# Weight rounding shared out by step, attention products moved and loads reordered in the first part of an attention and mixer kernel, and two products and some sums moved in the second

## The chip, the cores and the metric

One core of one Trainium2 chip. The metric is the device time of one execution in microseconds (us), lower is better. A kernel is executed several times and the median is quoted. Each comparison is made with executions of the kernel before on the same chip in the same rounds.

Ratios are computed as the mean time of one kernel's fast runs over the mean time of the other's fast runs of the same rounds, so they are not quite the ratio of the medians that are quoted. The brackets behind a ratio are its 95% interval.

## The reference, cut to what matters

```python
# 8 batches, 8 heads, 576 positions, head dimension 64; all in float32
kv  = einsum('bhsd,bhse->bhde', k, v)
out = einsum('bhsd,bhde->bhse', q, kv)
x   = out / sqrt(mean(out*out, -1) + 1e-6) * g_norm      # then heads side by side: (8, 576, 512)
# token mixing, w_tok1 (576, 256), w_tok2 (256, 576)
h = maximum(x.transpose(0, 2, 1) @ w_tok1, 0) @ w_tok2
u = x + h.transpose(0, 2, 1)
# channel mixing, w_ch1 (512, 1536), w_ch2 (1536, 512)
result = u + maximum(u @ w_ch1, 0) @ w_ch2
```

The four weight matrices arrive as float64, two 32-bit words for each value. The kernel has to turn them into float32 itself.

## The kernel before

The kernel has two parts. The first does attention and token mixing and stores `u`. It works on pairs of batches: after the attention of the first pair, a loop of three passes puts the attention of the next pair beside the token mixing of the last, and one more token mixing ends it. The second part does the channel mixing of nine groups, with two levels of fast matrix products (seven products instead of eight).

The steps of the first part have short names: `kv00` to `kv11` (k^T v of one batch, half of the heads), `a0` to `a3` (q times kv, with the norm), `r` (the 64 positions left over), `h00` to `h11` and `hr` (first token layer), `u0` to `u8` (second). The program issues them in a fixed order, and every engine works through its own instructions in that order.

A `kv` step ends with two short copies that pack the block for the next products, one on VectorE and one on ScalarE:

```python
def kv(side, half):
    acc = ps["kv"].tile([P, 2, P], F32, name="ps_kv")          # one such buffer
    ...                                                        # 20 matmuls
    keep(nc.vector.tensor_copy(dst[:HF, :, :D], acc[:HF, :, :D]))
    copy(dst[HF:, :, D:], acc[HF:, :, D:])                     # ScalarE
    load(n + 4)
```

An `a` step squares its product on ScalarE at once and leaves the rest for later (`due`): `mean` (VectorE's reduction, then the root on ScalarE) in the first half of the filling of its own step, `divide` in the second half, the gain on GpSimd after the next step:

```python
def mean():
    keep(nc.vector.tensor_reduce(ms, x3, axis=AX.X, op=ALU.add))
    ...
    keep(nc.scalar.activation(root, ms, AF.Sqrt))
def divide():
    ...
    keep(nc.vector.tensor_mul(x3, o, inv.to_broadcast([P, n * H, D])))   # frees ps_o, the one buffer
def gain(t):
    keep(nc.gpsimd.tensor_mul(xt, xt, g_sb.to_broadcast([P, H, D])))
```

The rounding of one block of weights is three fill steps. The first costs VectorE nothing; each of the others has one VectorE instruction with one input from SBUF and one with two:

```python
def scale():    # ScalarE L162, GpSimd L163
    keep(nc.scalar.activation(dst, hi.bitcast(F32), AF.Copy, scale=2.0 ** -112))
    keep(nc.gpsimd.tensor_scalar(out=dst, in0=dst, scalar1=TOP, scalar2=-TOP, op0=ALU.min, op1=ALU.max))
def upper():    # VectorE L168, L170
    keep(nc.vector.tensor_scalar(out=bits, in0=bits, scalar1=3, ..., op0=ALU.logical_shift_left))
    keep(nc.vector.scalar_tensor_tensor(out=bits, in0=hi, scalar=0x80000000, in1=bits, ...))
def lower():    # VectorE L176, L178, GpSimd L118
    keep(nc.vector.tensor_scalar(out=part.bitcast(U32), in0=bits, scalar1=0xFF800000, ...))
    keep(nc.vector.scalar_tensor_tensor(out=part, in0=lo, scalar=2.0 ** -52, in1=part, ...))
    tensor_add(dst, dst, part, engine=nc.gpsimd)
```

These fill steps are laid behind the steps of the loop, evenly:

```python
def run(body, fill):
    for n, step in enumerate(body):
        step()
        upto = len(fill) * (n + 1) // len(body)
        ...          # the fill steps up to `upto`, in two halves, each followed by what is due
```

In the profile, L127 is the helper through which every matmul goes, L118 that of the additions, L121 that of the relus, L124 that of ScalarE's copies, L283 VectorE's copy of kv, L298 the mean, L310 the multiplication that ends a norm. PSUM is the memory of this kernel's `ps_` tiles, SBUF that of its other tiles. A group of matmuls is called cold when it ran at a lower granted clock and so took longer than the same group elsewhere (4.64 us against 2.50 for the 20 matmuls of a `kv`), and warm otherwise.

## Time and profile before

| Stage of the profiled run | us |
|---|---|
| start: attention of the first pair | 0 to 53 |
| three passes of the loop | 53.6, 61.8, 60.6 |
| last token mixing | 40.6 |
| channel mixing, nine groups | 659.7 |
| whole (median of 3 runs 928.79, 928.31 to 930.03) | 929.3 |

The views behind this table are shown in the prediction. They are to be read by stage: in the channel mixing TensorE is busy nearly all the time, so only the few waits in it can be won. In the first part TensorE is busy 50 to 54 us of passes that take up to 61.8. What stands between is time in which it waits for a buffer or a packed block, plus the slow matmuls that follow some of the waits.

### The profile page before, as it was taken

What the parts mean: (1) busy time and instruction counts of PE and PEld (TensorE: products, weight loads), DVE (VectorE), ACT (ScalarE), POOL (GpSimd) and SP (SyncE); (2) the same over time, 40 slices, a digit from 0 to 9 for tenths busy, and PEclk for the clock granted to TensorE, in tenths of its full rate; (3) what the DMA queues carried; (4) which work ended last, traced back from release to release, by engine and by line L of the source; (5) the groups of instructions that cost most, each with busy time, mean ns of one, the idle gap of its engine ahead of it and who ended that gap; (6) DMA issues with size and microseconds to landing.
All of it is one profiled execution on the core that took longest, in us unless ns stands there. A gap on an engine that the chain in (4) does not pass through costs nothing.

```text
span 929.3 us, 12432 instructions
## 1 busy us (share of the span) xinstructions
PE 864.5 (93%) x5136; PEld 735.6 (79%) x5136; DVE 566.6 (61%) x862; ACT 175.8 (19%) x300; POOL 279.9 (30%) x164
## 2 busy tenths in 40 slices
PE   4589798898979998999999999999999999999997
PEld 4566365564458888889989989989989989989986
DVE  2747948769886577636726736636646646546652
ACT  2212122131201101301301311211310310220210
POOL 1534434444430003502502601700700800800710
PEclk9689989899989999999999999999999999999999
DMA  9976657715330011002002002002002002001001
GB/s 295 342 237 192 225 159 227 236 52 180 104 125 1 1 39 53 1 1 91 1 1 91 1 1 92 1 1 91 1 1 91 1 1 89 3 1 46 1 1 45
DMA packets 43576, 72.53 MB, mean 78 GB/s; under 512 B 2688, under 2 KB 21120, under 8 KB 43520
## 3 DMA queue, kind: packets, MB, share of 16 engines
q1 hardware_dynamic: 42160, 70.53, 23.0%
q10 hardware_dynamic: 1360, 1.21, 0.4%
q8 instruction: 40, 0.66, 0.3%
q14 instruction: 16, 0.13, 0.0%
HBM read 52.85 MB, written 18.87 MB: 77 GB/s over the span
## 4 chain that ended last, share of the span: by engine, by line
PE 78%; DVE 13%; issue 3%; ACT 2%; DMA 2%; SPq 0%; ACTq 0%; DVEq 0%
PE ps_w L127 34%; PE ps_v L127 31%; PE ps_h L127 6%; PE ps_kv L127 3%; DVE w_ch L170 2%; PE ps_o L127 2%; DMA v_in<-in_v_dram 2%; DVE x L118 2%; DVE ms L298 2%; PE ps_ut L404 2%; ACT v L121 1%; DVE w_ch L168 1%; DVE part L176 1%; DVE uT L118 1%; DVE x L310 1%
## 5 line engine op out<-in xcount | busy, mean ns | idle before, releaser
L127 PE MATMUL ps_v<-uT,w 128*128 128x128 f32 (+1 forms) x1656 | 213.2, 282 | 5.2 <-DVE uT L118 5.2
L127 PEld LDWEIGHTS ps_v<-uT,w 128*128 128x128 f32 x1656 | 200.9, 194 | 8.0 <-issue 5.6
L118 POOL TENSOR_TENSOR vs<-vs,v 128x1536 f32<-128x1536 f32 x8 | 27.7, 3467 | 422.9 <-DVE vs L118 422.9
L127 PE MATMUL ps_v<-uT,w_ch 128*128 128x128 f32 (+1 forms) x864 | 124.6, 287 | 4.0 <-DVE u L118 4.0
L127 PEld LDWEIGHTS ps_v<-uT,w_ch 128*128 128x128 f32 x864 | 112.7, 192 | 8.2 <-DVE u L118 4.4
L127 PE MATMUL ps_w<-w_ch,v 128*128 128x256 f32 x432 | 97.0, 381 | 5.6 <-ACT v L121 5.6
L127 PE MATMUL ps_w<-d,vs 128*128 128x256 f32 x432 | 96.2, 379 | 0.0
L127 PE MATMUL ps_w<-w_ch,vs 128*128 128x256 f32 x432 | 96.2, 379 | 0.0
L127 PEld LDWEIGHTS ps_w<-w_ch,v 128*128 128x128 f32 x432 | 80.8, 190 | 17.5 <-ACT v L121 7.1
L118 DVE TENSOR_TENSOR vs<-ps_v,u 128x384 f32<-128x384 f32 (+1 forms) x123 | 69.0, 561 | 39.3 <-PE ps_v L127 30.4
L127 PEld LDWEIGHTS ps_w<-w_ch,vs 128*128 128x128 f32 x432 | 81.5, 190 | 10.7
L127 PEld LDWEIGHTS ps_w<-d,vs 128*128 128x128 f32 x432 | 80.8, 190 | 10.3
L124 ACT COPY t<-ps_v 128x384 f32<-128x384 f32 (+1 forms) x59 | 28.6, 485 | 208.8 <-PE ps_v L127 196.6
L127 PEld LDWEIGHTS ps_kv<-v_in,k_in 128*128 128x128 f32 x320 | 44.7, 224 | 28.3 <-ACT kvp L124 11.4
L127 PE MATMUL ps_kv<-v_in,k_in 128*128 128x128 f32 x320 | 47.2, 312 | 21.4 <-DMA v_in<-in_v_dram 11.9
L127 PE MATMUL ps_u<-h,w_tok 128*128 128x512 f32 (+1 forms) x160 | 66.4, 602 | 0.0
L127 PE MATMUL ps_h<-x,w_tok 128*128 128x512 f32 (+1 forms) x160 | 66.2, 610 | 0.0
L118 DVE TENSOR_TENSOR u<-ps_v,t 128x384 f32<-128x384 f32 (+1 forms) x59 | 33.3, 565 | 46.1 <-PE ps_v L127 45.9
L118 POOL TENSOR_TENSOR w_ch<-w_ch,part 128x384 f32<-128x384 f32 (+1 forms) x28 | 35.1, 1254 | 84.3 <-DVE part L178 84.3
L118 POOL TENSOR_TENSOR v<-v,vs 128x1536 f32<-128x1536 f32 x16 | 55.3, 3454 | 12.9 <-DVE v L118 8.9
L118 DVE TENSOR_TENSOR u<-ps_w,u 128x512 f32<-128x512 f32 x18 | 12.5, 692 | 73.6 <-PE ps_w L127 73.6
L118 DVE TENSOR_TENSOR uT<-uT 128x512 f32<-128x512 f32 (+1 forms) x68 | 56.6, 874 | 0.6
(74 smaller groups left out, 995.1 us busy)
## 6 DMA issues: line engine op xcount, KB each, us to landing
qT<-in_q_dram SPq DMA_DIRECT2D x8, 1152.0 KB, 7.4
xg<-u_dram SPq DMA_DIRECT2D x9, 1024.0 KB, 5.7
k_in<-in_k_dram SPq DMA_DIRECT2D x16, 512.0 KB, 5.6
u_dram<-x SPq DMA_DIRECT2D x16, 512.0 KB, 3.1
out_dram<-xg SPq DMA_DIRECT2D x16, 512.0 KB, 2.8
v_in<-in_v_dram SPq DMA_DIRECT2D x14, 512.0 KB, 6.7
raw<-in_moe_w_ch_dram SPq DMA_DIRECT2D x16, 384.0 KB, 6.6
raw<-in_moe_w_ch_dram SPq DMA_DIRECT2D x12, 512.0 KB, 4.3
```

The source lines that it names most:

```text
L118: keep(engine.tensor_tensor(out=o, in0=a, in1=b, op=op))
L121: keep(nc.scalar.activation(o, a, AF.Relu))
L124: keep(nc.scalar.copy(o, a))
L127: keep(nc.tensor.matmul(*a, **kw))
L168: keep(nc.vector.tensor_scalar(out=bits, in0=bits, scalar1=3, scalar2=None, op0=ALU.logical_shift_left))
L170: keep(nc.vector.scalar_tensor_tensor(out=bits, in0=hi, scalar=0x80000000, in1=bits, op0=ALU.bitwise_and, op1=ALU.bitwise_or))
L176: keep(nc.vector.tensor_scalar(out=part.bitcast(U32), in0=bits, scalar1=0xFF800000, scalar2=None, op0=ALU.bitwise_and))
L298: keep(nc.vector.tensor_reduce(ms, x3, axis=AX.X, op=ALU.add))
L310: keep(nc.vector.tensor_mul(x3, o, inv.to_broadcast([P, n * H, D])))
L404: keep(nc.tensor.transpose(pt[:, c], xg[g][:, i, ts(c, P)], ident))
```

## The change

Its intent is to let VectorE do as much rounding in the loop as there is room for, in the steps where there is room, and to take away waits of TensorE. It has five parts:

1. The loads of k, v and q of the second pair go ahead of those of the token weights.
2. Rounding is shared out by step instead of evenly: six shares to an `h` step, four to a `kv`, one to a `u`, none to `a` and `r`. The loop rounds 27 blocks instead of 24, so three are left for the last token mixing instead of six. The three blocks rounded before the loop stand behind `r` and `a2` now, and no longer behind the steps from `a0` to `kv11`.
3. The attention products stand further apart among the other steps, and `a3` of the first pair moves behind the first `h00`.
4. In the channel mixing the order of two of the seven outer products, 5 and 2, is exchanged, with their relus.
5. The last eight sums of channel weights are done in the first group instead of the second.

Cut to its core:

```diff
-    ORDER = (1, 6, 7, 5, 2, 3, 4)
+    ORDER = (1, 6, 7, 2, 5, 3, 4)
 ...
-    def run(body, fill):
+    def run(body, fill, shares=None):
+        shares = shares or [1] * len(body)
 ...
-            upto = len(fill) * (n + 1) // len(body)
+            upto = len(fill) * sum(shares[:n + 1]) // sum(shares)
 ...
-    second = "h00 kv00 h01 kv01 a0 h10 h11 hr kv10 a1 kv11 u0 u1 r u2 a2 u3 u4 u5 u6 a3 u7 u8"
+    middle = ("h10 h11 a1 hr kv10 u0 kv11 u1 a2 u2 r u3 u4 u5 a3 u6 u7 u8").split()
+    second = "h00 kv00 h01 kv01 a0".split() + middle
 ...
+    share = {"h": 6, "k": 4, "u": 1, "a": 0, "r": 0}
 ...
-    for n in (0, 1, 2):
-        blocks[n][0]()            # loads of token weights
-    load(2)
-    load(3)
-    load_q(1)
-    for n in (3, 4):
-        blocks[n][0]()
+    for n in range(2, 4):
+        load(n)
+    load_q(1)
+    for n in range(5):
+        blocks[n][0]()
 ...
-    run(steps[2:6], [blocks[0][1], blocks[1][1]] + weights[:9])
+    run(steps[:6], [])
+    run(steps[6:], [b[1] for b in tok1] + [f for b in tok1 for f in b[2:]])
 ...
-    cut = 3 * 27
-    run(steps, weights[9:cut])
+    cut = 3 * 27 + 2
+    names = ["h00", "a3"] + second[1:] + 2 * both
+    run([...], weights[:cut], [share[name[0]] for name in names])
 ...                                # channel mixing, first group
-            weave([...], sums[:-8])
+            weave(body[:11], sums)
```

More of the change, by code (lines that the diff above doesn't have):

```diff
@@ L526, in after5 @@
             padd(s3, s3, s1)
-            relus.append((3, do(relu, a22, a22)))
+            relus.append((4, do(relu, a22, a22)))
         def after2():
             padd(a11, a11, s4)
-            relus.append((4, do(relu, a11, a11)))
+            relus.append((3, do(relu, a11, a11)))
         def after4():
@@ L665, in staggered @@
     def staggered(blocks, ahead=5):
-        steps = []
+        steps = [blocks[0][1], blocks[1][1]]
         for n, (_, _, upper, lower) in enumerate(blocks):
@@ L702 @@
                       ap=[[0, P], [0, 1], list(g_norm.ap[0])]), nc.scalar)
-    first = "kv00 kv01 a0 kv10 a1 kv11 r a2 a3"
-    second = "h00 kv00 h01 kv01 a0 h10 h11 hr kv10 a1 kv11 u0 u1 r u2 a2 u3 u4 u5 u6 a3 u7 u8"
-    both = "kv00 h00 kv01 h01 a0 h10 h11 hr kv10 a1 kv11 u0 u1 r u2 a2 u3 u4 u5 u6 a3 u7 u8"
+    first = "kv00 kv01 a0 kv10 a1 kv11 r a2"
+    middle = ("h10 h11 a1 hr kv10 u0 kv11 u1 a2 u2 r u3 u4 u5 a3 u6 u7 u8").split()
+    second = "h00 kv00 h01 kv01 a0".split() + middle
+    both = "kv00 h00 kv01 h01 a0".split() + middle
     last = "h00 h01 h10 h11 hr u0 u1 u2 u3 u4 u5 u6 u7 u8"
+    share = {"h": 6, "k": 4, "u": 1, "a": 0, "r": 0}
     blocks = ([get_tok1(0, 2), get_tok1(2, 2), get_tok1(4, 1)] + [get_tok2(t) for t in range(NTOK)]
@@ L711 @@
               + [get_ch2(f) for f in range(NF)])
-    weights = staggered(blocks)
-    for n in (0, 1, 2):
-        blocks[n][0]()
-    load(2)
-    load(3)
-    load_q(1)
-    for n in (3, 4):
-        blocks[n][0]()
-    steps = steps_of(first, attention(0))
-    run(steps[:2], [])
-    run(steps[2:6], [blocks[0][1], blocks[1][1]] + weights[:9])
-    run(steps[6:], [])
-    steps = []
-    for pair in range(B // 2 - 1):
-        steps += steps_of(both if pair else second, attention(pair + 1), token_mixing(pair))
-    cut = 3 * 27
-    run(steps, weights[9:cut])
+    for n in range(2, 4):
[3 more added lines that the diff above has]
+        blocks[n][0]()
+    tok1, blocks = blocks[:3], blocks[3:]
+    attention_0 = attention(0)
+    steps = steps_of(first, attention_0)
+    run(steps[:6], [])
+    run(steps[6:], [b[1] for b in tok1] + [f for b in tok1 for f in b[2:]])
+    for n in range(2, 5):
+        blocks[n][0]()
+    weights = staggered(blocks)
+    cut = 3 * 27 + 2
+    names = ["h00", "a3"] + second[1:] + 2 * both
+    at = [0, 0] + [0] * (len(second) - 1) + [1] * len(both) + [2] * len(both)
+    stages = [(attention(n + 1), token_mixing(n)) for n in range(B // 2 - 1)]
+    run([steps_of("a3", attention_0)[0] if n == 1 else steps_of(name, *stages[i])[0]
+         for n, (name, i) in enumerate(zip(names, at))],
+        weights[:cut], [share[name[0]] for name in names])
     left.close()
@@ L758 @@
             sums += [step for o in ORDER for step in mix_ch1_of(o)]
-            weave([step for pair in zip(channel2(g), extra + [lambda: None]) for step in pair],
-                  sums[:-8])
+            body = [step for pair in zip(channel2(g), extra + [lambda: None]) for step in pair]
+            weave(body[:11], sums)
+            for step in body[11:]:
+                step()
             continue
-        weave(channel1(g), sums[-8:] + [lambda: None] * 14 if g == 1 else [])
+        for step in channel1(g):
+            step()
         for n, step in enumerate(channel2(g)):
```

## The prediction

> **What bounds the kernel now.** I read four views in this order: the busy time by stretches, cut at the borders of the program's stages; the waits of TensorE; the timeline of TensorE; the timelines of VectorE, ScalarE and GpSimd around the waits found. The stretches (us; busy time and instructions of PE, PEld, DVE, ACT, POOL; clock; DMA share; GB/s):
>
> ```profile
> 0.00:53.00 53.00, 27.85 (x161) 26.32 (x162) 25.45 (x46) 11.13 (x19) 19.11 (x29) 0.76 1.01 315
> 53.00:106.60 53.60, 50.33 (x240) 30.12 (x239) 38.54 (x70) 13.26 (x26) 22.04 (x21) 0.98 0.62 197
> 106.60:168.40 61.80, 53.70 (x242) 33.66 (x240) 45.12 (x83) 12.77 (x26) 25.70 (x27) 0.92 0.65 212
> 168.40:229.00 60.60, 52.95 (x243) 32.76 (x241) 45.65 (x80) 13.59 (x26) 27.73 (x25) 0.94 0.42 136
> 229.00:269.60 40.60, 35.39 (x107) 16.18 (x105) 37.03 (x53) 7.61 (x14) 17.54 (x14) 0.97 0.39 137
> 269.60:344.20 74.60, 74.60 (x344) 65.37 (x345) 46.53 (x70) 10.16 (x17) 2.72 (x1) 0.97 0.06 22
> 344.20:384.50 40.30, 35.42 (x295) 34.65 (x293) 29.69 (x52) 9.45 (x16) 20.79 (x6) 0.96 0.11 41
> 384.50:929.30 544.80, 534.31 (x3514) 496.53 (x3514) 298.59 (x413) 97.81 (x157) 144.31 (x42) 1.00 0.08 28
> ```
>
> The first row is the attention of the first two batches, with saturated DMA; the next three are the loop (attention of the next two batches beside token mixing of two); then the last token mixing; after 269.6 the channel mixing of nine groups, where TensorE is nearly full. So 660 us are close to TensorE's own bound and the room is in the first 270. There, TensorE's waits are (us in total, times, longest):
>
> ```profile
> PE ps_o L127 <- DVE x L310: 15.0, 4, 5.2
> PE ps_kv L127 <- DMA v_in<-in_v_dram: 11.9, 2, 6.6
> PE ps_kv L127 <- ACT kvp L124: 9.6, 3, 5.1
> PE ps_r L127 <- ACT kvp L124: 7.2, 1, 7.2
> ```
>
> Only the DMA line is data. The others are PSUM buffers (ps_o and ps_kv have one each) or packed kv blocks that VectorE had not got to. The waits cost more than they last, and the timeline shows it:
>
> ```profile
> 117.67 4.64 PE L127 MATMUL ps_kv<-v_in,k_in 128*128 128x128 f32 x20 [5.10 <-ACT kvp L124]
> 136.88 2.50 PE L127 MATMUL ps_kv<-v_in,k_in 128*128 128x128 f32 x20
> 161.42 3.47 PE L127 MATMUL ps_o<-kvp,qT 128*128 128x128 f32 x16 [3.00 <-DVE x L310]
> 185.48 1.95 PE L127 MATMUL ps_o<-kvp,qT 128*128 128x128 f32 x16
> ```
>
> The same 20 matmuls take 4.64 us after a wait and 2.50 warm. In the channel mixing the waits are few:
>
> ```profile
> PE ps_w L127 <- ACT v L121: 5.6, 8, 0.9
> PE ps_v L127 <- DVE uT L118: 5.2, 1, 5.2
> PE ps_v L127 <- DVE u L118: 4.0, 2, 2.1
> ```
>
> What feeds the first of these lines is one relu on ScalarE that ends as TensorE starts:
>
> ```profile
> 383.05 1.49 ACT L121 ACTIVATE v<-v 128x1536 f32<-128x1536 f32 x1
> 384.58 5.45 PE L127 MATMUL ps_w<-w_ch,v 128*128 128x256 f32 x24 [0.95 <-ACT v L121]
> ```
>
> **What the Trainium skill says.** "TensorE: Matmul & The Clock Gate", Part 1: after an idle window of about 3.4 us TensorE falls to half clock, and needs about as long busy to come back. The trace agrees in kind (4.64 against 2.50; the granted clock is 0.92 in the second pass of the loop), though a wait of 2.99 us at 101.06 was followed by a 2.05 us group: near the limit it is chance. "PSUM — Partial Sum Buffer", Engine vs sequencer instructions: the queues of ScalarE, VectorE and GpSimd are strictly first in, first out. So work put ahead of a short copy delays that copy; the trace agrees: at 116.99 a 0.28 us copy of kv runs only after normalization, additions and rounding queued before it, and TensorE idles 5.1 us for it. "SBUF — State Buffer", SBUF: two separate sides: a VectorE instruction with two SBUF inputs and a GpSimd instruction exclude each other for their whole length. The trace agrees: the two-input rounding step takes 0.56 to 1.52 us for the same 384 columns.
>
> **The change, part by part.**
>
> 1. *Loads.* k, v, q of both batches now go ahead of the 1.18 MB of token weights. kv10's data landed at 21.7 behind 5.9 MB (297 GB/s in the first 25 us). Now it is behind 4.7 MB: 4.7/0.297 + 1.9 = about 17.8. The weights land at about 29 instead of 16. First kv waits for DMA cannot change.
>
> 2. *Start.* No rounding is put into the first six steps. Worked forward from the trace's durations: kv10 17.9 to 22.5, a1 to 25, kv11 to 27.4; VectorE ends a1's normalization (4.4 us after its square at 26.2) at 30.6, copies kv11 to 30.9; r to 32, a2 to 35. VectorE then has r's norm (3 us), rounding of two weight blocks (about 5.5) and GpSimd a 1.3 us addition: h00 starts at about 42.5, the deferred a3 ends at about 49. Before, a3 and h00 were both done at 57.4. Gain about 8.
>
> 3. *Loop.* Warm TensorE work of one pass from the timeline: four kv 2.25, four h 3.44, hr 1.9, four a 1.8, r 1.0, nine u about 16 in sum: 48.9. The passes took 53.6, 61.8, 60.6, the excess being waits of 3.3, 8.1, 7.7 and the cold clock after them. VectorE's work of one pass: four norms of 3.5, one of 2.3, nine additions of 0.64, four copies of 0.28, together 23.2; plus blocks. The fill goes from 72 steps to 83, 24 blocks to 27, so 9 to 9.2 a pass instead of 8; a block costs 2.4 to 2.9 (four instructions: 0.45, 1.15, 0.35, 0.56, and more at 512 columns). That is 46 to 50: VectorE becomes as full as TensorE. But it is now placed: 3 fill steps in each h, 2 in each kv, half of one in each u, none in a and r. Up to and with kv10 TensorE has 26.0 and VectorE 21 steps of 0.8 + two norms of 3.8 (with their gaps) + copies = 25.2; from u0 on 22.9 against 21.3. Balanced halves, and a2 and a3 stand 8.1 us apart, so a3 should no longer wait for ps_o, and kv01 of the next pass no longer for the backlog. What I expect left is one wait: kv11 needs ps_kv back from kv10's copy, only one u (1.76) lies between, and my step table has VectorE reach that copy 4 us after kv10 ends: 2.7 us of wait, more with the wider blocks of the third pass. Passes: about 49 (from 49 to 98), 52.5 and 55. Gains 0.5 (its saving is partly in point 2), 9, 5.5.
>
> 4. *Last token mixing.* Three blocks are left for it instead of six: VectorE loses about 9 of its 37 us, TensorE's own work is 33.4 with transposes and the first products of the next stage. The 5.2 us wait for uT shrinks to about 1.3 (an addition, half a block, two sums stay behind the last u). Gain 4, and some 1.5 at the cold start of the next stage.
>
> 5. *Order of outer products (5 and 2 exchanged) in channel mixing.* The relu of the first operand of the second layer moves one product (4.69 us) earlier; 8 waits, 5.6 us, go. In exchange GpSimd's four additions of 3.45 start later: the last ends at 457.4 instead of 456.2, and two sums of VectorE (3.6) make s2 ready at 461.06, where TensorE wants it at 461.4. It fits by 0.3 us. Gain 5.6.
>
> 6. *Sums of channel weights all in the first group.* VectorE has about 4.9 us of work for each 5.6 us product there, so it fits. The group after it took 39.4 against 32.8 for the next: gain 6.6 (4.0 of waits, the rest cold clock).
>
> Sum: 8 + 0.5 + 9 + 5.5 + 4 + 1.5 + 5.6 + 6.6 = 40.7, that is 888; I say 890, as VectorE has no slack left for mishaps.
>
> **Rivals.**
>
> *Rival A: VectorE becomes the bound of the loop.* For it: 46 to 50 us of work plus the gaps of five norms (about 0.3 each at the root). If the rounding meets GpSimd more often (1.5 instead of 0.6 us for the two-input step), a pass takes 57 and the loop gains 9 us less: about 900. Against: the h steps hold no gain multiplications, which are the other GpSimd work.
>
> *Rival B: the start only exchanges waits.* The later token weights could hold h00 as long as the attention did. If they land at 36 and not 29, the gain of part 2 falls to about 3: 895. For it: DMA share 1.01 in that stretch, and SyncE issues in order. Against: the rate rises to 344 GB/s after 25 us, and VectorE's queue reaches them only after 33.
>
> *Rival C: the new order makes TensorE wait for s2.* With the margin of 0.3 us a little jitter costs up to 1 us in each of eight groups, and 5.6 becomes nothing: about 896.
>
> *Rival D: kv11's wait is long enough for the cold clock* in each pass: 3 x 3 us more: about 899. For it: only one u lies between. Opposite: if no wait stays, passes of 50 give about 881.
>
> **Range and chances.** Parts 5 and 6 rest on waits with known causes (12 us). Parts 2 to 4 (28 us) rest on a table of steps; half of it could fail. A gain of 18.6 is needed for 2%, and parts 5, 6 and half of 2 alone nearly reach it. Prediction 890, range 879 to 904; faster 0.95, within 2% 0.04, slower 0.01.
>
> **What would show each step.** 1, 2: kv10 starts near 18, h00 near 42, a3 done near 49. 3: borders of the passes near 98, 150 and 205; no wait of ps_o for the normalization; one wait of ps_kv for the copy in each pass; VectorE above 85% busy in the passes. 4: wait for uT below 2 us. 5: no line of ps_w waiting for ScalarE, none for VectorE's vs. 6: the second group's first layer takes about 33. The prediction is wrong if a pass still takes 58 or more with VectorE's busy time risen alike, or if h00 starts after 50.

## The result, and the profile after

The changed kernel is correct. It takes 915.57 us (median of 4 runs, 913.54 to 918.69) against 929.41 (928.31 to 930.94) before: ratio 0.9853 [0.9821, 0.9885]. That is a gain of 1.5%, within the 2% that counts as the same, and 12 us outside of the predicted range of 879 to 904.

By stages, in the profiled runs (us from the start of the run):

| Border | before | predicted | measured |
|---|---|---|---|
| kv10 of the first pair starts | 21.8 | 17.9 | 18.8 |
| first h00 starts | 52.8 | 42.5 | 41.9 |
| first pass ends | 106.6 | 98 | 113.0 |
| second pass ends | 168.4 | 150 | 169.2 |
| third pass ends | 229.0 | 205 | 230.1 |
| channel mixing starts | 269.6 | 242 | 267.8 |
| end | 929.3 | 890 | 916.9 |

The profiled run of the changed kernel was the slowest of its four. One second kv group in its start met a cold clock, so its h00 is late: in the other profiles with the same loads that step starts between 37.4 and 40.3. Read the borders with that margin of 2 to 4 us.

The stretches of the changed kernel, from the end of `a3` on (columns: length; busy time and instructions of PE, PEld, DVE, ACT, POOL; clock; DMA share; GB/s). The rows are the three passes, the last token mixing, the first group of the channel mixing, the first layer of the second group, and the rest:

```profile
54.10:113.00 58.90, 49.43 (x234) 31.14 (x232) 47.81 (x81) 13.87 (x28) 27.59 (x24) 0.94 0.62 195
113.00:169.20 56.20, 51.87 (x242) 31.71 (x240) 48.49 (x84) 13.29 (x28) 28.05 (x27) 0.94 0.73 234
169.20:230.10 60.90, 52.92 (x242) 31.96 (x240) 53.43 (x89) 15.39 (x29) 32.97 (x28) 0.92 0.44 142
230.10:267.80 37.70, 35.44 (x106) 16.16 (x104) 26.38 (x35) 5.10 (x9) 9.26 (x7) 1.00 0.33 118
267.80:341.50 73.70, 73.67 (x342) 64.60 (x343) 49.62 (x79) 9.57 (x16) 0.00 (x0) 0.98 0.04 16
341.50:376.40 34.90, 34.29 (x299) 33.64 (x298) 22.89 (x39) 8.78 (x16) 18.66 (x6) 1.00 0.15 50
376.40:916.90 540.50, 534.21 (x3516) 495.99 (x3514) 299.96 (x415) 98.46 (x157) 146.90 (x43) 1.00 0.08 28
```

Two things are to be seen. The channel mixing takes 649.1 (267.8 to 916.9) instead of 659.7: a gain of 10.6 us, the larger part of what the whole kernel gained. And the first part, where the prediction had two thirds of the gain, ends 1.8 us earlier only. Its start is better; the first pass, from where h00 starts to its end, has become 17 us longer (71.1 for 53.8, the moved a3 in it: 3.7 us of matmuls after a wait of 2.4), and that has eaten the start.

The waits of TensorE in the first part (us in sum, times, longest) are no longer those of before:

```profile
PE ps_kv L127 <- ACT kvp L124: 10.1, 5, 4.0
...
PE ps_u L127 <- ACT h L121: 6.7, 3, 3.3
PE ps_h L127 <- POOL w_tok L118: 5.8, 1, 5.8
PE ps_o L127 <- DVE x L310: 5.6, 3, 2.9
PE ps_o L127 <- ACT kvp L124: 5.5, 2, 5.3
```

`ps_o` waiting for the norm went from 15.0 to 5.6, as intended. In its place stand a wait of `u` for the relus of `h` (6.7), which the kernel before didn't have among its larger ones, and a wait of `a0` for the packed kv block (5.3 once). The first line names ScalarE's copy, but a kv block is packed by two copies and the release is put down to the last; VectorE's, which stands in a longer queue, is the one to look at.

In the channel mixing, from 290 on, only this is left:

```profile
PE ps_v L127 <- DVE u L118: 0.5, 1, 0.5
PE ps_w L127 <- DVE vs L118: 0.4, 1, 0.4
```

**Where the passes lose it: the second pass, near 135 to 147.** VectorE first (start, duration, engine, line, operation, out<-in; what stood before it in brackets):

```profile
135.13 1.51 DVE L178 SCALAR_TENSOR_TENSOR part<-raw,part 128x384 f32<-128x384 uint32 x1
136.56 1.42 DVE L168 TENSOR_SCALAR w_ch<-w_ch 128x384 uint32<-128x384 uint32 x1
138.02 1.24 DVE L170 SCALAR_TENSOR_TENSOR w_ch<-raw,w_ch 128x384 uint32<-128x384 uint32 x1
139.18 1.21 DVE L298 TENSOR_REDUCE ms<-x 128x16 f32<-128x1024 f32 x1
...
145.47 0.27 DVE L283 COPY kvp<-ps_kv 64x128 f32<-64x128 f32 x1
```

ScalarE in the same stretch:

```profile
140.63 0.22 ACT L301 ACTIVATE root<-ms 128x16 f32<-128x16 f32 x1 [4.43 <-DVE ms L299]
140.75 2.04 ACT L121 ACTIVATE h<-ps_h 128x512 f32<-128x512 f32 x4
```

And TensorE:

```profile
136.93 2.50 PE L127 MATMUL ps_kv<-v_in,k_in 128*128 128x128 f32 x20
141.38 2.44 PE L127 MATMUL ps_u<-h,w_tok 128*128 128x512 f32 x4 [1.96 <-ACT h L121]
146.15 4.13 PE L127 MATMUL ps_kv<-v_in,k_in 128*128 128x128 f32 x20 [2.32 <-ACT kvp L124]
```

The chain is: rounding holds VectorE, so a1's mean is reduced only at 139.18. ScalarE's root waits for it (4.43 us idle). The relus of `h` have nothing to do with that root, but they stand behind it in ScalarE's queue, so they start at 140.75 and u0 waits 1.96 us. Then VectorE, still behind, comes to kv10's copy at 145.47, and kv11 waits 2.32 us. Neither wait is long, but kv11's matmuls after the second one take 4.13 us instead of 2.50. The granted clock fell behind the first wait already: it is 0.79 from 141.4 to 143.8, in u0's matmuls, and 0.50 from there to 149. The multiplication that GpSimd did meanwhile is the reason that the roundings at 135 are so long:

```profile
134.85 2.92 POOL L314 TENSOR_TENSOR x<-x,g_sb 128x512 f32<-128x512 f32 x2
```

While it runs, the two VectorE instructions that begin at 135.13 and 136.56 take 1.51 and 1.42 us; the shortest of the same two kinds and size in this trace take 0.56 and 0.34.

**Where the first pass loses it: near 60 to 68.** VectorE, where the blocks are token weights, 576 columns wide:

```profile
59.29 0.27 DVE L283 COPY kvp<-ps_kv 64x128 f32<-64x128 f32 x1
...
59.96 1.72 DVE L170 SCALAR_TENSOR_TENSOR w_tok<-raw,w_tok 128x576 uint32<-128x576 uint32 x1
...
64.32 1.83 DVE L170 SCALAR_TENSOR_TENSOR w_tok<-raw,w_tok 128x576 uint32<-128x576 uint32 x1
...
67.55 0.28 DVE L283 COPY kvp<-ps_kv 64x128 f32<-64x128 f32 x1
```

TensorE finished kv01 at about 62.4 and then had the part of a0 that needs only the first block; the rest had to wait:

```profile
68.22 2.93 PE L127 MATMUL ps_o<-kvp,qT 128*128 128x128 f32 x12 [5.31 <-ACT kvp L124]
```

Between the two copies lie two whole blocks of rounding, about 8 us of VectorE without a gap. TensorE has 6.1 us of work in the same place (h01 3.60, kv01 2.50). That makes about half of the wait of 5.31. The other half was lost before: kv00's own copy, at 59.29, came 2.8 us after kv00 had ended (56.5), as it stands behind the norm of the moved a3 on VectorE.

The late start of this profile hides one more wait. In the runs with the same loads and shares whose start was on time (experiments 2, 5 and 6), ScalarE comes to the scaling of the first channel-weight block before the data is there, and waits 9.5 us for it, until about 52. The square of a3 stands behind that scaling on ScalarE, and a3's norm and kv00's copy behind the square, so kv01 waits 3.7 to 3.8 us for its buffer. Here a3's matmuls end at 54.3, after the scaling at 52.27, and it costs nothing.

### The profile page after: what moved, and what is told of

Read it like the earlier page. It is cut to its first block, busy times and chain, and to the rows that moved or that the text cites. A ratio compares the mean times of both kernels' runs of the same rounds, so it can differ in the third digit from the quotient of the medians.

```text
span 916.9 us, 12416 instructions
## 1 busy us (share of the span) xinstructions
PE 865.6 (94%) x5136; PEld 733.7 (80%) x5136; DVE 572.3 (62%) x862; ACT 175.8 (19%) x300; POOL 281.7 (31%) x164
## 4 chain that ended last, share of the span: by engine, by line
PE 78%; DVE 14%; issue 3%; DMA 2%; ACT 1%; SPq 1%; POOL 0%; POOLq 0%; DVEq 0%; ACTq 0%
PE ps_w L127 34%; PE ps_v L127 31%; PE ps_u L127 4%; PE ps_kv L127 3%; PE ps_o L127 2%; DMA v_in<-in_v_dram 2%; DVE w_ch L170 2%; PE ps_h L127 2%; PE ps_ut L404 2%; DVE ms L298 2%; DVE x L310 1%; DVE part L176 1%; DVE w_ch L168 1%; DVE uT L118 1%; DVE x L118 1%
## 5 line engine op out<-in xcount | busy, mean ns | idle before, releaser
L127 PE MATMUL ps_v<-uT,w 128*128 128x128 f32 (+1 forms) x1656 | 210.3, 280 | 2.4 <-DVE uT L118 2.3
L127 PEld LDWEIGHTS ps_v<-uT,w 128*128 128x128 f32 x1656 | 198.4, 192 | 4.8 <-issue 2.7
L127 PE MATMUL ps_u<-h,w_tok 128*128 128x512 f32 (+1 forms) x160 | 69.0, 615 | 6.8 <-ACT h L121 6.7
L314 POOL TENSOR_TENSOR x<-x,g_sb 128x512 f32<-128x512 f32 x36 | 49.1, 1382 | 62.6 <-DVE x L310 46.9
L127 PEld LDWEIGHTS ps_kv<-v_in,k_in 128*128 128x128 f32 x320 | 46.7, 233 | 27.0 <-ACT kvp L124 15.7
L127 PE MATMUL ps_kv<-v_in,k_in 128*128 128x128 f32 x320 | 49.3, 322 | 17.0 <-ACT kvp L124 10.1
L118 DVE TENSOR_TENSOR u<-ps_v,t 128x384 f32<-128x384 f32 (+1 forms) x59 | 33.3, 564 | 46.0 <-PE ps_v L127 45.9
L118 POOL TENSOR_TENSOR v<-v,vs 128x1536 f32<-128x1536 f32 x16 | 55.1, 3445 | 19.9 <-DVE v L118 10.5
L127 PEld LDWEIGHTS ps_h<-x,w_tok 128*128 128x128 f32 (+1 forms) x160 | 27.4, 196 | 37.3 <-issue 28.9
```

Of the source, the lines that this page charges most:

```text
L118: keep(engine.tensor_tensor(out=o, in0=a, in1=b, op=op))
L127: keep(nc.tensor.matmul(*a, **kw))
```

## The experiments

My theory after reading these two traces: the channel mixing gives its 10 us as predicted, and the shares are what takes the rest back, since they put more rounding into the first half of a pass than VectorE can do there. The rivals were that the new places of the attention products do it (through the relu that now stands behind a root), that the later token weights do it, and that VectorE's total load does it wherever the rounding is placed. Sixteen kernels were run. Fourteen were correct and timed; two gave a wrong result.

| Experiment | us, median (range) | Ratio to before |
|---|---|---|
| the change itself | 915.57 (913.54–918.69) | 0.9853 [0.9821, 0.9885] |
| parts 4 and 5 alone | 919.84 (918.56–920.99) | 0.9886 [0.9866, 0.9905] |
| old places | 911.52 (909.28–913.62) | 0.9800 [0.9778, 0.9823] |
| even shares | 906.13 (905.97–907.42) | 0.9746 [0.9731, 0.9761] |
| old loads | 915.31 (913.87–920.01) | 0.9850 [0.9819, 0.9881] |
| a1 after hr | 916.34 (915.08–916.69) | 0.9858 [0.9836, 0.9880] |
| u1 before kv11 | 913.37 (912.91–914.29) | 0.9828 [0.9802, 0.9855] |
| no gain (wrong result) | 902.27, one run | – |
| no rounding (wrong result) | 883.10, one run | – |
| shares 2-2-1 | 907.94 (906.95–912.34) | 0.9777 [0.9748, 0.9806] |
| shares 2-2-1, two blocks later | 903.67 (903.17–908.66) | 0.9734 [0.9704, 0.9764] |
| even shares, old places | 908.99 (906.12–911.30) | 0.9788 [0.9765, 0.9810] |
| first h00 one share | 914.51 (913.42–915.36) | 0.9837 [0.9822, 0.9852] |
| the same, two blocks later | 908.19 (907.47–909.65) | 0.9771 [0.9753, 0.9788] |
| the same, and old places | 904.99 (904.49–905.19) | 0.9735 [0.9720, 0.9749] |
| even shares, two blocks later | 911.99 (910.34–913.83) | 0.9805 [0.9788, 0.9822] |
| 2-2-1, two blocks later, old places | 906.04 (904.08–907.65) | 0.9740 [0.9722, 0.9758] |

### 1. Parts 4 and 5 alone

The kernel before, with the new order of the outer products and all sums in the first group.

```diff
-    ORDER = (1, 6, 7, 5, 2, 3, 4)
+    ORDER = (1, 6, 7, 2, 5, 3, 4)
-            relus.append((3, do(relu, a22, a22)))
+            relus.append((4, do(relu, a22, a22)))
-            relus.append((4, do(relu, a11, a11)))
+            relus.append((3, do(relu, a11, a11)))
-            weave([...], sums[:-8])
+            weave(body[:11], sums)
```

> The kernel before with the parts of the channel mixing alone (order of outer products, sums all in the first group). Theory (the channel mixing gave the whole gain, the first part of the program gave under 2 us): channel mixing from 659.7 to about 649, time about 918.5, that is 10.5 us under the kernel before. Rival (the two halves of the change share the gain): about 922.

Measured: 919.84 against 929.93 before. About 10 of the roughly 14 us are these two small edits. All that was done to the first part together brings 3 to 4.

### 2. Old places of the attention products

The changed kernel with the old order of steps in the middle of a pass.

```diff
-    middle = ("h10 h11 a1 hr kv10 u0 kv11 u1 a2 u2 r u3 u4 u5 a3 u6 u7 u8").split()
+    middle = ("h10 h11 hr kv10 a1 kv11 u0 u1 r u2 a2 u3 u4 u5 u6 a3 u7 u8").split()
```

> The changed kernel, with the attention products of a pass back in their old places; shares and loads as changed. Theory (a1 just ahead of hr puts the root of its norm ahead of the relus of h on ScalarE and its norm ahead of kv10's copy on VectorE): waits of u0 for the relu of h (6.7 us in three passes) go, waits of kv11 for the copy (9 us) fall under 3; a wait of a3 for ps_o of some 2 us a pass comes back; time about 908. Rival 1 (VectorE's load as a whole bounds the pass): the waits move elsewhere, time within 2 us of the changed kernel's 915.6. Rival 2 (the further places do help): slower, 920.

Measured: 911.52, some 4 us shorter than the changed kernel (ratios 0.9800 against 0.9853). The wait of `u` for the relus is gone, but that of `ps_kv` for the packed block grew from 10.1 to 16.4 (3.7 of it is kv01's wait in the first pass, which the profile of the changed kernel hides). So the new places cost a little beside these shares, and do not explain the missing 25.

### 3. Even shares

The changed kernel, with every step given the same amount of rounding.

```diff
-    share = {"h": 6, "k": 4, "u": 1, "a": 0, "r": 0}
+    share = {"h": 1, "k": 1, "u": 1, "a": 1, "r": 1}
```

> The changed kernel, with the rounding steps spread evenly over the 69 steps of the loop again (1.2 a step). Theory (the shares put 7 of 9 blocks of a pass into its first half, where VectorE then needs more than TensorE's 26 us): kv11's and u0's waits shrink from 16 us to about 5, a3's waits for ps_o grow to 3 us a pass; time about 912 to 916. Rival 1 (shares are what little helps): slower by 5 us or more, 921. Rival 2 (only the load counts): no change.

Measured: 906.13, 9.4 us shorter than the changed kernel. This is the main finding: of the parts of the change, the sharing out is what loses time. Its first two passes in the profile:

```profile
48.40:97.50 49.10, 46.62 (x234) 28.42 (x232) 41.43 (x74) 14.22 (x28) 24.87 (x25) 1.00 0.75 250
97.50:156.40 58.90, 52.43 (x242) 32.24 (x240) 45.88 (x85) 12.98 (x27) 26.51 (x28) 0.94 0.69 226
```

The first pass takes 49.1, as predicted for the changed kernel, instead of 58.9, at full clock; it ends at 97.5, and the changed kernel's at 113.0 (110 to 111 in experiments 5 and 6). VectorE in the same place as above, the copies of kv00 and kv01:

```profile
53.53 0.28 DVE L283 COPY kvp<-ps_kv 64x128 f32<-64x128 f32 x1
...
56.75 0.28 DVE L283 COPY kvp<-ps_kv 64x128 f32<-64x128 f32 x1 [1.78 <-PE ps_kv L127]
```

Now only half a block lies between them, and it is VectorE that waits for TensorE (1.78 us). a0 waits 0.28 us instead of 5.31. The later passes are not better than those of the changed kernel (58.9 and 61.4), so even shares are not right there either: kv01 waits 4.5 and 4.1 us in them. Nor is a block cheaper: over these two passes the four rounding instructions take 12.48 + 20.75 + 8.89 + 13.83 = 55.95 us for 18.5 blocks, 3.02 each. What the even spread changes is where the fill steps stand: the rounding on VectorE, and the scaling on ScalarE, which no longer waits for data in the first pass here.

### 4. Old loads

The changed kernel with the first token weights ahead of k, v and q again.

```diff
-    for n in range(2, 4):
-        load(n)
-    load_q(1)
-    for n in range(5):
-        blocks[n][0]()
+    for n in range(3):
+        blocks[n][0]()
+    for n in range(2, 4):
+        load(n)
+    load_q(1)
+    for n in range(3, 5):
+        blocks[n][0]()
```

> The changed kernel, with the three loads of first token weights ahead of k, v, q of the second batch again. Theory (a start bounded by VectorE after 31 us and by kv10's data before): kv10 starts 3 to 4 us later (22 instead of 18.8), half of it is hidden behind the wait of h00 for its weights: time 1 to 2 us longer than the changed kernel. Rival (weights that come late are what holds h00 at 41.9): h00 starts earlier and the time falls by 3.

Measured: 915.31, no different. kv10 starts at 22.0 again and h00 at 41.9, yet the first pass ends at 109.8, where it ends at 110 to 111 in the two next experiments with the new loads. So part 1 of the change is worth nothing beside these shares: what it gains is spent in the first pass. The traces show where. VectorE's copy of kv00 comes at 57.66 here, and at 57.05 and 57.46 in experiments 5 and 6, though h00 started 4 us earlier there. There a3's square waits on ScalarE behind the channel weights until about 52; here a3 itself is done only then.

### 5. a1 after hr

The changed kernel, with a1 moved behind the step whose relus it held back.

```diff
-    middle = ("h10 h11 a1 hr kv10 u0 kv11 u1 ...
+    middle = ("h10 h11 hr a1 kv10 u0 kv11 u1 ...
```

> The changed kernel, with a1 and hr exchanged in each pass (a1 directly after hr), so that on ScalarE the four relus of h stand ahead of the square and the root of a1. Theory (u0 waits because the relus queue behind a root that waits for VectorE): u0's waits for the relu of h, 6.7 us in sum, go; kv11 still waits for kv10's copy, as a1's norm stays ahead of it on VectorE: that wait grows by what u0 no longer takes, time 0 to 4 us shorter. Rival (the relu's wait costs in itself): 7 us and more shorter, about 908.

Measured: 916.34, no gain. The wait of `u` for the relus is gone, which shows that the root in front of them was its cause. But `ps_kv`'s wait for the packed block rose from 10.1 to 21.2 us (3.8 of it is again kv01's, hidden in the other profile). With VectorE behind, the time was only waited for elsewhere.

### 6. u1 before kv11

The changed kernel, with two `u` steps between kv10 and kv11, so that kv10's copy has more time.

```diff
-    middle = ("h10 h11 a1 hr kv10 u0 kv11 u1 a2 ...
+    middle = ("h10 h11 a1 hr kv10 u0 u1 kv11 a2 ...
```

> The changed kernel, with u1 ahead of kv11, so that two products of token mixing stand between kv10 and kv11. Theory (kv11 waits for kv10's copy, which VectorE reaches 2 to 4 us late): the wait of kv11 falls from 2.3 to 4.0 us a pass to under 1.5, time about 4 us shorter (911). Rival (VectorE's backlog meets TensorE at the next place, a2): same time.

Measured: 913.37, some 2 us shorter. The wait that the prediction had named can be shortened so, but a2 now waits for kv11's block: 2.26, 2.38 and 0.20 us in the three passes.

### 7. No gain

The changed kernel without GpSimd's multiplications by `g_norm`. The result is wrong; one execution.

```diff
-            due[now[0] + 1, 0] += [do(gain, t) for t in range(n)]
+            pass
```

> Wrong result on purpose: the changed kernel without GpSimd's multiplication by the gain (36 of 1.38 us). It tells what the meeting of GpSimd and VectorE costs. Theory (a rounded block costs VectorE 3.1 to 3.4 us in the passes, and not 2.6, because its two-input steps wait for GpSimd): blocks fall to about 2.6, VectorE's first half of a pass by 4 us, waits of kv11 and u0 by half, first part of the program 8 to 12 us shorter: about 905. Rival (GpSimd's multiplications cost nothing, VectorE's queue alone decides): within 2 us of the changed kernel.

Measured: 902.27. Passes 59.4, 51.6 and 55.0. The second pass:

```profile
106.85:158.43 51.58, 49.22 (x243) 30.10 (x241) 42.16 (x85) 13.72 (x27) 15.27 (x18) 1.00 0.79 259
```

The second and third pass now take what the prediction gave them (52.5 and 55). The four rounding instructions of VectorE take 7.90 + 19.08 + 7.90 + 11.30 = 46.2 us for 18 blocks of these two passes, 2.57 a block. In the changed kernel they take 10.71 + 23.01 + 10.11 + 13.97 = 57.8 for 18, or 3.21. The run also takes a step out of the way of `x`, but no wait of TensorE in the loop of the changed kernel names that multiplication.

The first pass is not helped, so its loss has another cause. Its longest wait here is kv01's, 5.77 us: ScalarE waits 10.56 us for the first channel weights, with a3's square behind. The wait of a0, 5.31 in the changed kernel, is 0.87.

### 8. No rounding

The changed kernel with `upper` and `lower` returning at once, so that VectorE and GpSimd are left with their fixed work and the scaling. The result is wrong; one execution.

```diff
         def upper():
+            return
         def lower():
+            return
```

> Wrong result on purpose: the changed kernel without the rounding on VectorE and GpSimd's addition for it (the scaling stays). It tells what a pass takes when VectorE is not loaded. Theory (VectorE's rounding is what feeds the waits inside the passes): passes of 50 to 51 us instead of 58.9, 56.2, 60.9, wait for the first token weights shorter, time about 885. Rival (the chain of a norm, square, mean, root, division, and the single ps_o and ps_kv hold the pass by themselves): passes of 54 and more, time above 897.

Measured: 883.10. Passes 60.1, 48.94 and 48.95. The first of them misses the 50 to 51 by far, with no rounding at all, and ends at 100.1, later than the first pass of experiment 3 (97.5), which has all its rounding. The wait for data on ScalarE does it; its scaling and TensorE's kv01:

```profile
51.91 0.54 ACT L162 ACTIVATE w_ch<-raw 128x384 f32<-128x384 f32 x1 [14.98 <-DMA raw<-in_moe_w_ch_dram]
57.99 4.22 PE L127 MATMUL ps_kv<-v_in,k_in 128*128 128x128 f32 x20 [12.19 <-ACT kvp L124]
```

So the first pass has two causes that stand one behind the other, this and the rounding in front of the copies. The second pass:

```profile
100.10:149.04 48.94, 48.94 (x242) 30.16 (x240) 23.59 (x49) 13.59 (x27) 16.36 (x19) 1.00 0.83 270
```

TensorE is busy in all of it, 48.94 us, and VectorE 23.59. The prediction's table had 48.9 and 23.2. Both fixed sums were right; what was wrong is the rounding beside them.

### 9. Shares 2-2-1

A flatter sharing out: two for `h` and `kv`, one for `u`.

```diff
-    share = {"h": 6, "k": 4, "u": 1, "a": 0, "r": 0}
+    share = {"h": 2, "k": 2, "u": 1, "a": 0, "r": 0}
```

> The changed kernel, with shares 2 for h and kv, 1 for u, 0 for a and r, instead of 6, 4, 1, 0, 0: 16 to 17 of 28 steps of a pass fall before u0 instead of 21; evenly spread it was 12. Theory (a step costs VectorE 1.0 to 1.1 us and not 0.8, so 6-4-1 overfills the half before u0 and the even spread the half after it; the best lies between): both kv01's wait of 4.5 us of the even spread and the waits of u0 and kv11 of 6-4-1 shrink; time about 902, under the even spread's 906. Rival (any placing that favours h harms): between 906 and 915.

Measured: 907.94, passes 52.9, 56.0 and 60.6. I had hoped for 902: a miss. It is better than 6-4-1 and no better than even.

### 10. Shares 2-2-1, two blocks fewer in the loop

As 9, and two of the 27 blocks left for the last token mixing.

```diff
-    cut = 3 * 27 + 2
+    cut = 3 * 25 + 2
```

> As the run with shares 2, 2, 1, and two more of the 30 blocks left for the last token mixing (5 instead of 3). Theory (with blocks of 3.1 us VectorE has some 52 us of work a pass for TensorE's 48.9; the last token mixing has 11 us of VectorE to spare): each pass 2 us shorter, last stage 0 to 2 longer: 898. Rival (the last stage has no room, as in the kernel before with its six blocks): no gain, 902 or more.

Measured: 903.67, 4 us better than 9 (though one slow execution in each makes the ranges overlap), passes 49.1, 55.1 and 58.8. What is left for later is paid in part: the last token mixing takes 40.6 and the wait for uT is 4.5 us again (2.3 in the changed kernel).

### 11. Even shares, old places

As 3, with the old order in the middle.

```diff
-    middle = ("h10 h11 a1 hr kv10 u0 kv11 u1 ...
+    middle = ("h10 h11 hr kv10 a1 kv11 u0 u1 ...
```

> The changed kernel with the even spread and the old places of the attention products, that is without both of the two changes inside the passes. Theory (the further places pay once VectorE is not overfilled before u0): slower than the even spread with the new places (906), about 911, with a wait of a3 for ps_o of some 3 us a pass. Rival (the new places are harmful whatever the shares): faster, 902 or less.

Measured: 908.99, some 3 to 4 us longer than 3 (ratios 0.9788 against 0.9746). With even shares the new places help; `ps_o` waits for the norm 19.0 us in sum with the old ones. In experiment 2, with 6-4-1, the same exchange went the other way. The places are good or bad only together with what is between them.

### 12. First h00 with one share

A second theory for the first pass: the six shares of the very first h00 bring a scaling step to ScalarE that waits there for data which is still on its way, and everything behind it waits along.

```diff
-        weights[:cut], [share[name[0]] for name in names])
+        weights[:cut], [1] + [share[name[0]] for name in names[1:]])
```

> The changed kernel, with a share of 1 instead of 6 for the very first step of the loop (h00 of the first pass); everything else as changed. The scaling of the first channel-weight block then stands on ScalarE behind the copy of kv00 and no longer ahead of the square of a3. Theory (the first pass lost its time because that scaling waits 6 to 10 us on ScalarE for a block that lands at 52, behind the k, v, q put ahead of it, and a3's norm, kv's copies and the token weights' rounding queue up behind): first pass from 59-63 down to about 53, time 907 to 910. Rival (the mass of rounding in the first h and kv steps does it, whatever the data): time within 2 us of 915.6.

Measured: 914.51; I had expected 907 to 910. The theory fell: ScalarE's wait for data is gone from the trace, yet the first pass takes 61.2, and a0 still waits:

```profile
61.25 2.93 PE L127 MATMUL ps_o<-kvp,qT 128*128 128x128 f32 x12 [4.20 <-ACT kvp L124]
```

Between kv00's copy (53.44) and kv01's (60.58) VectorE now waits 1.89 us for a block to be scaled, and then rounds one whole block, four instructions of 1.52, 1.70, 0.81 and 0.93, stretched by a gain multiplication on GpSimd from 55.53 to 58.24. With two blocks it was 8 us, here it is 7 for one: what stands between the copies is still longer than TensorE's 6.1. Later in the same pass u0 waits 2.11 for the relus and kv11 4.27 for kv10's copy, as in the changed kernel. So the wait for data is not what holds the pass by itself: with it gone, what is put in front of the copies takes its place. With neither (experiment 3) the pass takes 49.1.

### 13. The same, two blocks fewer in the loop

As 12, with a smaller cut.

```diff
-    cut = 3 * 27 + 2
+    cut = 3 * 25 + 2
```

> As the run with one share for the first h00, with two more blocks left for the last token mixing. Theory (VectorE has about 53 us of work a pass for TensorE's 49): passes two and three each 2 us shorter, last stage 2 us longer: 2 to 4 us under the run with one share alone, about 904. Rival (only placing counts): same time as that run.

Measured: 908.19, 6 us better than 12, passes 55.9, 54.1 and 59.6.

### 14. The same, with old places

As 13, with the old order in the middle.

```diff
-    middle = ("h10 h11 a1 hr kv10 u0 kv11 u1 ...
+    middle = ("h10 h11 hr kv10 a1 kv11 u0 u1 ...
```

> As the run before it, with the attention products back in their old places. Theory (with 6-4-1 the new place of a1, just ahead of hr and kv10, is bad, as the run with old places alone said, 4 us): about 900, the best of all. Rival (the old places only helped the first pass, by chance of its queue): 904 or more.

Measured: 904.99, passes 54.5, 54.5 and 56.0. I had expected 900. Old places win 3 us beside 6-4-1 again, as in experiment 2.

### 15. Even shares, two blocks fewer in the loop

As 3, with a smaller cut. Fewer blocks had helped twice, so I expected the same here.

```diff
-    cut = 3 * 27 + 2
+    cut = 3 * 25 + 2
```

> The changed kernel with the even spread and two more blocks left for the last token mixing. Theory (VectorE's load of a pass stands beside placing as a second cause): under the even spread alone (906.1) by the 4 to 6 us that the same step gave at 2-2-1 and at 6-4-1, so 901 to 902, the best of all. Rival (the even spread has already what fewer blocks give): 905 to 906.

Measured: 911.99, 6 us worse than 3: a clear miss. The passes take 53.5, 58.7 and 56.6 and the last token mixing 45.9, against 49.1, 58.9, 61.4 and 39.1 in experiment 3. The third pass gained 4.8; the first lost 4.4 and the last token mixing 6.8. There TensorE waits 2.63 us for an addition of VectorE (1.22 in experiment 3), the next 32 matmuls take 15.56 us instead of 12.48, and the wait for uT is 4.5 us instead of 2.3. Two lines of VectorE in the first pass show why the count alone doesn't decide:

```profile
73.38 1.50 DVE L170 SCALAR_TENSOR_TENSOR w_ch<-raw,w_ch 128x384 uint32<-128x384 uint32 x1
...
76.73 0.28 DVE L283 COPY kvp<-ps_kv 64x128 f32<-64x128 f32 x1
```

And TensorE after them:

```profile
77.41 4.64 PE L127 MATMUL ps_kv<-v_in,k_in 128*128 128x128 f32 x20 [3.61 <-ACT kvp L124]
```

Other counts cut the list of fill steps at other places. Here a whole block falls in front of kv10's copy; in experiment 3 it was half a block, the copy came at 73.75, and kv11 waited 0.67 us and ran warm. Three microseconds of rounding at a wrong place cost 3 us of wait and 2 of cold clock there.

### 16. Shares 2-2-1, two blocks fewer, old places

As 10, with the old order in the middle.

```diff
-    middle = ("h10 h11 a1 hr kv10 u0 kv11 u1 ...
+    middle = ("h10 h11 hr kv10 a1 kv11 u0 u1 ...
```

> Shares 2-2-1, two more blocks left for the last token mixing, old places. The old places gained 3 to 4 us at 6-4-1 and lost 3 at the even spread, so between them I expect no difference from the run with the new places: 903 to 904. Rival (old places are better whenever h is favoured at all): 900.

Measured: 906.04 (904.08 to 907.65) beside 903.67 (903.17 to 908.66) of 10: no sure difference.

The best versions are experiments 10 and 14, 0.9734 and 0.9735 of the kernel before. They can't be told apart from each other, nor surely from 3 and 16 (0.9746 and 0.9740), and both beat the kernel before and the changed one.

## Why the prediction was right or wrong

**Steps 1 and 2, loads and start: right in time, wrong in worth.** kv10 started at 18.8 (predicted 17.9) and h00 at 41.9 (42.5), and up to 4 us earlier in other profiles. a3 was done at 54.1 (49), in a profile with one cold group; without it the first pass starts between 47.4 and 49.1 in the other profiles with these loads and with rounding. But experiment 4 shows that an earlier start doesn't shorten the kernel here: the first pass behind it waits for the channel weights on ScalarE, and then for VectorE. I had added the 8 us to the sum as if the next stage would hand them on.

**Step 3, the loop: this is the step that failed**, and the term is the cost of rounding: "21 steps of 0.8" for the half of a pass up to kv10, from a block of 2.4 to 2.9 us. Measured is 3.21 us a block over the second and third pass (3.06 in the second, 3.36 in the third, with its wider blocks), so 1.07 for each of its three steps. With 1.07, an estimate, that half holds 21 x 1.07 + 7.6 (two norms) + 0.8 (copies), about 31 us of VectorE against TensorE's 26. The halves were not balanced but 5 us apart: VectorE came to kv10's copy 5.4, 6.0 and 9.8 us after kv10 had ended, and not 4. Passes two and three came out 3.7 and 5.9 us above the prediction (56.2 and 60.9 for 52.5 and 55). Experiment 7 takes the gain multiplications away: 2.57 a block, within what I had assumed, and the two passes are 51.6 and 55.0. The prediction's own sign of being wrong came true: two passes took 58 or more, with VectorE's busy time up from 38.5 to 47.8 and from 45.7 to 53.4.

The working had the cause in sight and priced it out. Rival A says that the two-input step may meet GpSimd more often, and that passes then take 57; against it I put that the `h` steps "hold no gain multiplications". That was wrong by the kernel's own text: a gain is due one step after its norm, and the step after a0 is h10. In the trace it lies beside roundings accordingly (134.85 above, before a1's mean at 139.18). Rival A, with 900, was the nearest of them, and still too low.

The first pass, 9.9 us over the prediction, is only in part this term. The average over half a pass hid that five fill steps stand between the copies of kv00 and kv01, and four of them are the rounding of two whole blocks. At 2.4 a block that is 4.8 us, less than the 6.1 of TensorE beside them, and no wait follows. They took about 8 us: these are the widest blocks (576 columns), and they were stretched besides (1.83 us for an instruction that takes 0.76 in experiment 3). The wait was 5.3, half of it from the norm of a3 before them. Experiments 3 and 12 bracket it: with half a block there the wait is 0.28; with a wait for scaling and one stretched block, 7 us in all, it is 4.20.

The other part was not in the working: the shares put the scaling of the first channel weights on ScalarE ahead of a3's square, and their data comes at about 52. Experiments 7 and 8 leave that wait, and their first pass stays at 59.4 and 60.1; 12 takes only that wait away and stays at 61.2; 3 has neither that wait nor two blocks in front of the copy and takes 49.1.

One more wait was not in the step table: u0 behind the relus, which stand behind a root, which waits for VectorE (6.7 us in sum). It came from step 3's new place of a1, and experiment 5 confirms the chain. It isn't the cause of the missing time, since taking it away gained nothing.

The wait that I did foresee, kv11 for kv10's copy, came out near its size by luck: 2.7 predicted; 2.73, 2.32 and 4.03 in the three passes. VectorE was later than predicted, and u0's wait before it (1.41, 1.96 and 3.34) took up the difference. That the matmuls behind it start cold (rival D) came true, but in the second and third pass the clock had fallen behind u0's wait already.

**Step 4, last token mixing: nearly right.** 37.7 against 36.5; the wait for uT 2.3 against 1.3 (5.2 before).

**Steps 5 and 6, channel mixing: right.** All waits for ScalarE's relu went. The new order made TensorE wait for the vector sums 0.4 us, once, so rival C fell: the margin of 0.3 us held. The first layer of the second group took 34.9 by the stretches' borders, against 40.3; predicted was a gain of 6.6, measured 5.4. The rest of the channel mixing, where the order of the products counts, gained 4.3 of the predicted 5.6. Together 10.6 of the 13.7 that steps 5, 6 and the warm start were given, and experiment 1 shows about 10 for the two alone.

**Rival B**, the later token weights, fell with experiment 4: loads in either order give the same time.

What stays open: what the new place of a3 costs in the first pass, since its norm stands ahead of kv00's copy in every run with the changed start; the exact share of each wait in the first pass of the changed kernel, since taking one away moved it (experiments 5 and 6), and a rule for how many blocks fit. Two blocks fewer gave 4 and 6 us in two versions and cost 6 in a third. That the place of single steps before a short copy decides it was seen in the traces of experiments 3 and 15, but I did not build a kernel that moves just that one step.

## What to carry to other kernels

When filler work is shared out over an engine's queue, size it by what it costs while the other engines run, and check it in front of each short instruction that another engine waits for; an average over half a stage hides a queue of 8 us before a copy of 0.28. Ask also whether the data of each filler step is there when its turn comes: here one scaling step ahead of its data held back everything behind it on ScalarE. When two engines are equally full, taking away one wait mostly moves it, so measure the parts of such a change separately: here two small edits brought 10 us, while the sharing out, in the middle of three other edits, lost 9. And time won ahead of a stage counts only if that stage is not bound by something else.

## What the Trainium skill lacked or had wrong

- "TensorE: Matmul & The Clock Gate", Part 1: the rule there is one idle window of about 3.4 us. The same part says that frequent short idle times between groups can make the clock oscillate too, but not how short. Here the granted clock was down to 0.50 after a wait of 1.96 us and 2.44 us of matmuls, and a group after another wait of 2.32 us took 4.13 us instead of 2.50. At the same place in experiment 4, waits of 1.72 and 2.78 us with 1.98 us of matmuls between them left the clock at 1.00. In experiment 10 a single wait of 1.90 us (at 158.3, clock 1.00 before it) was followed by 0.50 and a group of 4.13. So the length of a wait alone did not decide it here.
- "SBUF — State Buffer", SBUF: two separate sides: the rule that a VectorE instruction with two SBUF inputs and a GpSimd instruction that reads SBUF exclude each other agrees with these traces (1.51 against 0.56 us for one rounding instruction). Its clause on one-input instructions in a two-port mode fits too (1.42 against 0.34), if this one runs in such a mode, which no view shows. What it lacks is what this makes of a mixed stream: here a block of four such instructions took 2.57 us without the gain multiplications beside it and 3.21 with them, a quarter more.
- "PSUM — Partial Sum Buffer", Engine vs sequencer instructions: that ScalarE's queue is strictly first in, first out agrees. No page that I read draws the consequence that cost 6.7 us of waits here: a small instruction that waits for another engine (the root, 0.22 us) holds back the unrelated relus behind it, and through them TensorE.
